# Six transfers of a gated attention and MLP kernel split by rows: 120 and 8, 8 and 56

## The chip, the cores and the metric

The kernel runs on one core of one Trainium2 chip. The core has five engines with an instruction stream each: TensorE (PE, with weight loads shown as PEld), VectorE (DVE), ScalarE (ACT), GpSimd (POOL) and SyncE (SP). Data goes between the chip's main memory (HBM) and the core's on-chip memory of 128 partitions in transfers that an engine's queue issues and that 16 DMA engines carry out. The metric is the time of one execution in device microseconds (us); lower is better.

## The reference

One token with 640 features goes through an attention block with 32 heads over a cache of 4,096 keys and values of 128 numbers, and through an MLP of 1,728 units with the mish activation. A gate mixes the two. What is wanted is the output and, for a given gradient of it, the gradients of x, of both caches, of both attention weights, of the MLP's three arrays and of the gate:

```python
def _fwd_reference(A_x, A_k_cache, A_v_cache, A_wq, A_wo, B_x, B_w1, B_b1, B_w2, gate_w):
    def _A_ref(x, k_cache, v_cache, wq, wo):
        B, Sq, D = x.shape
        H, Dh = 32, 128
        q = (x @ wq).reshape(B, Sq, H, Dh) -> (B, H, Sq, Dh)
        scores = jnp.einsum("bhqd,bhkd->bhqk", q, k_cache) * (Dh ** -0.5)
        p = _softmax(scores, axis=-1)
        o = jnp.einsum("bhqk,bhkd->bhqd", p, v_cache)
        return o -> (B, Sq, H * Dh) @ wo
    def _B_ref(x, w1, b1, w2):
        h = jnp.einsum("bsd,df->bsf", x, w1) + b1
        sp = jnp.log1p(jnp.exp(-jnp.abs(h))) + jnp.where(h > 0, h, jnp.zeros_like(h))
        return jnp.einsum("bsf,fd->bsd", h * jnp.tanh(sp), w2)
    g = _sigmoid((x * gate_w).sum(-1, keepdims=True))
    return g * _A_ref(...) + (1 - g) * _B_ref(...)

def reference(..., grad_out):
    out, vjp = jax.vjp(_f, A_x, A_k_cache, A_v_cache, A_wq, A_wo, B_w1, B_b1, B_w2, gate_w)
    return (out, *vjp(grad_out))
```

All arrays are bf16. Each head reads 1 MB of K and 1 MB of V and writes 1 MB of each one's gradient, 82.03 MB read and 82.03 MB written in all.

## The kernel before, in words

The work goes head by head, in an order written out by hand (the tile pools only hand out buffers and place the waits). A head's K and V lie as 128 partitions of 32 keys, 8,192 bytes to a partition. For a head h the loop turns V into its transposed form (`v_tr`: PE transposes of 128x128 into PSUM, ACT copies them out), works out the softmax and the gradient of the probabilities, turns K of head h+1 (`k_tr`), forms the gradient of V as an outer product on DVE (`dv_out`), then the scores of head h+1, and column sums over K and V (`dq_o`). The gradient of K follows one head later (`dk_out`). Both products go through the pool `outs` with four buffers `o_sb` of 1 MB, from which SP stores them.

K has four buffers and V three. So after `dq_o(h)`, which is the last to read the buffers of head h, `load_k(h + 4)` and `load_v(h + 3)` are issued. Nearly all transfers are issued by SP in the order of the program: in each head the two stores of products, the load of K, the load of V, and at some heads those of the weights wq and wo (in groups of four heads) and the stores of their gradients, which were written over the weights' own tiles. SP stands in this order: a transfer that has to wait holds up those behind it. Each transfer reports its landing on one of eight completion semaphores, which all HBM transfers of SP and ACT take in turn, so that a transfer also waits for the landing of the one that had its semaphore before.

The MLP's work is spread over the heads by a list with costs (`mq`). Its gradient of w2 (`dw2`) is written over the tile `w2_sb`: 13 columns of 128 rows, and 64 rows that are left over (F is 1,728 = 13 x 128 + 64). It is stored at head H - 4 = 28 in three pieces of 128 partitions and one piece of the 64 rows, 1,280 bytes each (line 725). The gradients of b1 (one row, `dh_bc`) and of w1 are stored at head 30, and three small stores of five rows each (`fin_rows`) end the kernel's compute, two of them issued by ACT and one by POOL. The last four stores are the halves of the two products of head 31, 512 KB each (line 580).

Lines of the page: L504 transposes, L505 copies from PSUM, L510 scores and gradient of the probabilities, L569 outer products, L582 their stores, L111 and L116 the loads of K and V, L592 column sums.

Of the kernel before, what the change touches and what calls it, by code (L numbers as in the profile page):

```python
# [16 lines left out]
def kernel(  # L17
# [24 lines left out]
    nc = tc.nc  # L42
    P = 128
    _, H, Sk, Dh = A_k_cache.shape
    D = A_x.shape[-1]
    F = B_w1.shape[1]
# [6 lines left out]
    FR = F // P  # L53
    FM = FR * P
    FT = F - FM
# [10 lines left out]
    Kv = A_k_cache.rearrange("b h (p j) d -> (b h) p j d", p=P)  # L66
    Vv = A_v_cache.rearrange("b h (p j) d -> (b h) p j d", p=P)
# [37 lines left out]

    kts, vts, wqs, wos = {}, {}, {}, {}

    def load_k(h):
        if h < H:
            kts[h] = kv_in.tile([P, J, Dh], BF16, name="Kn", tag="Kn")  # L110
            nc.sync.dma_start(kts[h][:], Kv[h])  # L111

    def load_v(h):
        if h < H:
            vts[h] = kv_in.tile([P, J, Dh], BF16, name="Vn", tag="Vn", bufs=VBUFS)
            nc.sync.dma_start(vts[h][:], Vv[h])  # L116

    wqp = {}

# [40 lines left out]
    w2_sb = const.tile([P, FCN, D], BF16, name="w2_sb")  # L160
# [83 lines left out]
    def g_do(g, hh):  # L244
        gp = groups[g]
        junk = small.tile([P, D], BF16, name="junk", tag="junk", bufs=2)
        nc.vector.scalar_tensor_tensor(junk[:], in0=wos[g][:, hh, :], scalar=1.0, in1=da_bc[:],  # L247
                                       op0=ALU.mult, op1=ALU.mult, accum_out=gp["do_col"][:, hh:hh + 1])
# [24 lines left out]
    def g_dobc(g):  # L273
        g_bcast(groups[g]["do_diag"], groups[g]["do_row"], 0, G)
# [16 lines left out]
    def f_bc(g, a=0, b=G):  # L291
        g_bcast(groups[g]["dq_diag"], groups[g]["dq_bc"], a, b)

    def f_o4(g):
        gp = groups[g]
        gp["o4"] = grp_sb.tile([P, G], F32, name="o4", tag="o4")
        ps = grp([P, G], F32, "o4_ps")
        nc.tensor.matmul(ps[:], lhsT=gp["o_sel"][:].rearrange("p h k -> p (h k)"), rhs=res[:], start=True, stop=True)
        nc.vector.tensor_copy(gp["o4"][:], ps[:])
        nc.vector.tensor_copy(gp["o_bf"][:], gp["o4"][:])  # L300
# [12 lines left out]
    def f_dx(g, c, a=0, b=G, slot=None):  # L313
        gp = groups[g]
        cs = slice(a * Dh, b * Dh)
        slot = g if slot is None else slot
        junk = small.tile([P, D], BF16, name="junk", tag="junk", bufs=2)
        nc.vector.scalar_tensor_tensor(junk[:, cs], in0=wqs[g][:, c, cs], scalar=1.0, in1=gp["dq_bc"][:, cs],  # L318
                                       op0=ALU.mult, op1=ALU.mult, accum_out=dx_parts[:, c, slot:slot + 1])
# [193 lines left out]
    def k_tr(h, c):  # L513
        if h < H:
            if c == 0:
                KT[h] = kvT.tile([P, J, P], BF16, name="KT", tag="KT")
            tr_block(kts[h], KT[h], c)

    def v_tr(h, c):
        if c == 0:  # L520
            VT[h] = kvT.tile([P, J, P], BF16, name="VT", tag="VT")
        tr_block(vts[h], VT[h], c)
# [11 lines left out]
    def softmax(h):  # L534
        mx = s_ps.tile([P, P + 2], F32, name="mx", tag="mx")
        nc.tensor.matmul(mx[:, 0:P], lhsT=scale_f[:], rhs=dgms.pop(h)[:], start=True, stop=True)  # L536
        negM = small.tile([P, 1], F32, name="negM", tag="negM")
        nc.vector.tensor_reduce(negM[:], mx[:, 0:P], axis=AX.X, op=ALU.max, negate=True)  # L538
        return mx, negM

    def exps(h, negM):
        es[h] = small.tile([P, J], BF16, name="e_bf", tag="e_bf")
        zds[h] = small.tile([P, 2], F32, name="zd", tag="zd")
        nc.scalar.activation(es[h][:], S_ps.pop(h)[:], ACT.Exp, bias=negM[:], scale=scale, accum_out=zds[h][:, 0:1])

    def dP(h):
        DP_ps[h] = s_ps.tile([P, J], F32, name="DP", tag="DP")
        cols_mm(DP_ps[h][:], VT.pop(h), doz[h // G % 2][:, h % G, :])
        pj = small.tile([P, J], F32, name="pj", tag="pj")
        nc.vector.scalar_tensor_tensor(pj[:], in0=DP_ps[h][:], scalar=1.0, in1=es[h][:],  # L550
                                       op0=ALU.mult, op1=ALU.mult, accum_out=zds[h][:, 1:2])

    def zd_mm(h, mx):
        nc.tensor.matmul(mx[:, P:P + 2], lhsT=ones_f[:], rhs=zds[h][:], start=True, stop=True)  # L554

    def probs(h, mx):
        rz = small.tile([P, 1], F32, name="rz", tag="rz")
        nc.vector.reciprocal(rz[:], mx[:, P:P + 1])
        negD = small.tile([P, 1], F32, name="negD", tag="negD")
        nc.vector.tensor_scalar(negD[:], mx[:, P + 1:P + 2], rz[:], -1.0, ALU.mult, ALU.mult)  # L560
        p4s[h] = p4b[h % 3][:, 0:J * 4].rearrange("p (j t) -> p j t", t=4)
        nc.vector.tensor_scalar(p4s[h], es.pop(h)[:].unsqueeze(2).to_broadcast([P, J, 4]), rz[:], None, ALU.mult)
        ds4s[h] = ds4b[h % 3][:, 0:J * 4].rearrange("p (j t) -> p j t", t=4)
        nc.vector.scalar_tensor_tensor(ds4s[h], in0=DP_ps.pop(h)[:].unsqueeze(2).to_broadcast([P, J, 4]),
                                       scalar=negD[:], in1=p4s[h], op0=ALU.add, op1=ALU.mult)
        zds.pop(h)
# [20 lines left out]
    def dk_out(h):  # L587
        out_pair(h, dKv, ds4s[h], groups[h // G]["qs_row"])
# [92 lines left out]
    for h in range(H - 1):  # L681
        g, hh = h // G, h % G
        nx, pv = g + 1 < NG, g > 0
        v_tr(h, 0)
        v_tr(h, 1)
        mx, negM = softmax(h)
        if h > 0:
            dk_out(h - 1)
        v_tr(h, 2)
        v_tr(h, 3)  # L690
        exps(h, negM)
        if hh == 0 and g == LG:
            g_dobc(g)
        dP(h)
        if hh == 0 and pv:
            f_o4(g - 1)
            f_bc(g - 1)
        k_tr(h + 1, 0)
        k_tr(h + 1, 1)
        zd_mm(h, mx)  # L700
        if hh == 0 and pv:
            f_dx(g - 1, 0)
        if hh == 1 and pv:
            f_dx(g - 1, 3)
        if hh == 2 and nx:
            g_do(g + 1, 0)
        if hh == 3 and nx:
            g_do(g + 1, 3)
        probs(h, mx)
        k_tr(h + 1, 2)  # L710
        if hh == 0 and pv:
            f_aT_pe(g - 1)
        k_tr(h + 1, 3)
        if hh == 3 and nx:
            g_dodiag(g + 1)
        dv_out(h)
        scores(h + 1)
        od = dq_o(h)
        load_k(h + KBUFS)
        load_v(h + VBUFS)  # L720
        if h == H - 4:
            assert dw2_next[0] == FCN
            for a, b in W2P:
                nc.sync.dma_start(dw2_v[:, a:b, :], w2_sb[:, a:b, :])
            nc.sync.dma_start(out_8[FM:F, :], w2_sb[0:FT, FR, :])
        if h == H - 2:
            assert not mq
            nc.sync.dma_start(db1_row, dh_bc[0:1, :])
            nc.sync.dma_start(dw1_v[:, 0:3, :], w1_sb[:, 0:3, :])
            nc.sync.dma_start(dw1_v[:, 3:RC, :], w1_sb[:, 3:RC, :])  # L730
        dqo_red(h, od)
        budget = 0.0
        if hh == 0:
            if nx:
                g_new(g + 1)
            if pv:
                f_aT_add(g - 1)
                f_dx(g - 1, 1)
                f_dx(g - 1, 2)
                f_dwo(g - 1, 0)  # L740
                f_dwo(g - 1, 1)
            budget = 0.9
        if hh == 1:
            if pv:
                f_dx(g - 1, 4)
                for c in range(RC):
                    f_dwq(g - 1, c)
                f_dwq_st(g - 1)
                f_dwo(g - 1, 2)
                f_dwo(g - 1, 3)  # L750
                f_dwo_st(g - 1)
            budget = 2.7
        if hh == 2:
            if nx:
                g_do(g + 1, 1)
                g_do(g + 1, 2)
                g_qcol(g + 1)
            budget = 0.9
        if hh == 3:
            if g % 2 == 0 and g + 2 < NG:  # L760
                load_wqp(g // 2 + 1)
            if g + 2 < NG:
                load_wo(g + 2)
            if nx:
                if g + 1 < LG:
                    g_dobc(g + 1)
                g_q(g + 1)
                g_qs(g + 1)
                g_docol(g + 1)
                f_new(g)  # L770
                f_diag(g)
            budget = 2.7
        if h >= 2:
            mlp_some(budget)
            dw2_some(2)

    g, h = NG - 1, H - 1
# [98 lines left out]
```

## Time and profile before

| | us |
|---|---|
| median of 3 runs | 415.16 (415.0 to 415.53) |
| the profiled execution | 416.13 |
| its span, first to last instruction | 414.4 |

| engine | busy us | share of the span |
|---|---|---|
| PE | 317.4 | 77% |
| DVE | 301.2 | 73% |
| ACT | 215.7 | 52% |
| POOL | 10.4 | 3% |

The granted clock of PE is 0.88 of full speed over the run. 164.05 MB go through SP's queue in the span. The 62 stores of whole products take 17.5 us (median) from issue to landing, the 32 loads of V 18.6, the loads of K 17.1. The longest waits of compute on a transfer: DVE's outer products on the stores that free their buffers 17.1 us in 10 waits, PE's transposes on V 3.5 us in 4 and on K 5.5 us in one, at the start.

How to read it: the page cuts the span into 40 slices of 10.36 us and gives for each the busy tenths of an engine, the share of the DMA engines in use and the GB/s that they moved. A queue's share is the time of its packets as a share of 16 engines' span. The chain of work that ended last goes back from the last instruction to what released it, step by step. In the timeline, a row is the start, the length and the instruction; SPq is SP issuing a transfer. Besides, the trace has for each completion semaphore the times of its single counts, and for every packet its start, length, size and queue; the number of the DMA engine is not in it.

### The profile page before, as it was taken

What the parts mean: (1) busy time and instruction counts of PE and PEld (TensorE: products, weight loads), DVE (VectorE), ACT (ScalarE), POOL (GpSimd) and SP (SyncE); (2) the same over time, 40 slices, a digit from 0 to 9 for tenths busy, and PEclk for the clock granted to TensorE, in tenths of its full rate; (3) what the DMA queues carried; (4) which work ended last, traced back from release to release, by engine and by line L of the source; (5) the groups of instructions that cost most, each with busy time, mean ns of one, the idle gap of its engine ahead of it and who ended that gap; (6) DMA issues with size and microseconds to landing.
All of it is one profiled execution on the core that took longest, in us unless ns stands there. A gap on an engine that the chain in (4) does not pass through costs nothing.

```text
span 414.4 us, 15457 instructions
## 1 busy us (share of the span) xinstructions
PE 317.4 (77%) x6839; PEld 285.2 (69%) x6839; DVE 301.2 (73%) x811; ACT 215.7 (52%) x447; POOL 10.4 (3%) x27
## 2 busy tenths in 40 slices
PE   4697995979859988888987876787978687879400
PEld 3497874878758886878777865777778685878400
DVE  2555872888689696999898885749899996886720
ACT  2364553755446445564567654774656445546600
POOL 3000001000000000000000002000000000000000
PEclk9998998989969798898989998987989898689855
DMA  8999999999999999999999999999999999999694
GB/s 273 406 413 422 419 422 422 407 420 419 421 421 420 418 419 421 411 420 419 422 420 423 416 404 411 409 417 423 422 416 375 411 394 414 403 391 377 278 346 168
DMA packets 31240, 165.05 MB, mean 398 GB/s; under 512 B 3012, under 2 KB 6725, under 8 KB 15174
## 3 DMA queue, kind: packets, MB, share of 16 engines
q1 hardware_dynamic: 30866, 164.05, 97.3%
q8 instruction: 53, 0.87, 0.8%
q14 instruction: 13, 0.11, 0.1%
q0 software_dynamic: 256, 0.01, 0.0%
q10 hardware_dynamic: 52, 0.01, 0.0%
HBM read 82.03 MB, written 82.03 MB: 396 GB/s over the span
## 4 chain that ended last, share of the span: by engine, by line
PE 32%; DMA 30%; DVE 17%; ACT 13%; issue 4%; DVEq 0%; ACTq 0%; SPq 0%
PE tr L504 14%; DMA out_dram<-o_sb 13%; DMA Vn<-in_A_v_cache_dram 10%; PE od L592 7%; DVE o_sb L569 6%; ACT KT L505 6%; DMA out_dram<-wo_g 5%; ACT VT L505 4%; PE DP L510 2%; PE S L510 2%; DVE junk L464 2%; PE q_ps L218 2%; DMA h_sb<-dh_bc 1%; DMA Kn<-in_A_k_cache_dram 1%; DVE junk L247 1%
## 5 line engine op out<-in xcount | busy, mean ns | idle before, releaser
L505 ACT COPY KT<-tr 128x512 f32<-128x512 f32 x128 | 69.8, 588 | 54.2 <-PE tr L504 54.1
L504 PE MATMUL tr<-ident_bf,Vn 128*128 128x128 bf16 x1024 | 80.3, 239 | 17.8 <-ACT VT L505 12.5
L504 PEld LDWEIGHTS <-Vn 128*128 128x128 bf16 x1024 | 71.8, 108 | 25.5 <-issue 20.1
L569 DVE TENSOR_TENSOR o_sb<-qs_row,ds 128x2048 bf16<-128x2048 bf16 x64 | 75.3, 1217 | 17.1 <-DMA out_dram<-o_sb 17.1
L505 ACT COPY VT<-tr 128x512 f32<-128x512 f32 x128 | 69.6, 584 | 27.4 <-PE tr L504 26.9
L504 PE MATMUL tr<-ident_bf,Kn 128*128 128x128 bf16 x1024 | 75.7, 230 | 7.0 <-DMA Kn<-in_A_k_cache_dram 5.5
L504 PEld LDWEIGHTS <-Kn 128*128 128x128 bf16 x1024 | 68.1, 105 | 12.0 <-DMA Kn<-in_A_k_cache_dram 5.5
L569 DVE TENSOR_TENSOR o_sb<-do_row,p 128x2048 bf16<-128x2048 bf16 x64 | 75.2, 1216 | 0.0
L532 ACT ACTIVATE dgm<-ident_bf,m 128x128 f32<-128x128 bf16 x32 | 12.9, 402 | 57.1 <-DVE m L530 57.1
L510 PE MATMUL DP<-doz,VT 128*128 128x32 bf16 x1024 | 36.3, 178 | 4.5 <-issue 2.1
L510 PE MATMUL S<-qz,KT 128*128 128x32 bf16 x1024 | 37.1, 180 | 3.1 <-ACT KT L505 0.4
L510 PEld LDWEIGHTS <-VT 128*128 128x128 bf16 x1024 | 31.7, 97 | 7.9 <-ACT VT L505 5.1
L510 PEld LDWEIGHTS <-KT 128*128 128x128 bf16 x1024 | 32.5, 98 | 6.5 <-ACT KT L505 5.6
L592 PE MATMUL od<-p,Vn 128*128 128x32 bf16 x1024 | 31.7, 179 | 3.7 <-issue 3.7
L554 PE MATMUL mx<-zd,ones_f 128*128 128x2 f32 x64 | 12.0, 258 | 25.9 <-DVE pj L550 25.7
L592 PEld LDWEIGHTS <-Vn 128*128 128x128 bf16 x1024 | 28.7, 97 | 4.1 <-issue 4.1
L592 PE MATMUL od<-ds,Kn 128*128 128x32 bf16 x1024 | 31.3, 180 | 0.1
L554 PEld LDWEIGHTS mx<-zd,ones_f 128*128 128x128 f32 x64 | 10.0, 197 | 28.8 <-DVE pj L550 28.8
L592 PEld LDWEIGHTS <-Kn 128*128 128x128 bf16 x1024 | 28.6, 98 | 0.2 <-issue 0.2
L247 DVE SCALAR_TENSOR_TENSOR junk<-wo_g,da_bc 128x640 bf16<-128x640 bf16 x32 | 25.4, 818 | 0.0
L318 DVE SCALAR_TENSOR_TENSOR junk<-wq_p,dq_bc 128x512 bf16<-128x512 bf16 x35 | 23.4, 684 | 0.7 <-ACT dq_bc L261 0.7
L538 DVE TENSOR_REDUCE negM<-mx 128x1 f32<-128x128 f32 x32 | 9.2, 286 | 17.5 <-PE mx L536 17.4
(162 smaller groups left out, 318.4 us busy)
## 6 DMA issues: line engine op xcount, KB each, us to landing
out_dram<-o_sb SPq DMA_DIRECT2D x62, 1024.0 KB, 17.5
Vn<-in_A_v_cache_dram SPq DMA_DIRECT2D x32, 1024.0 KB, 18.6
Kn<-in_A_k_cache_dram SPq DMA_DIRECT2D x31, 1024.0 KB, 17.1
wo_g<-in_A_wo_dram SPq DMA_DIRECT2D x8, 640.0 KB, 19.2
out_dram<-wo_g SPq DMA_DIRECT2D x7, 640.0 KB, 18.3
wq_p<-in_A_wq_dram SPq DMA_DIRECT2D x3, 1280.0 KB
out_dram<-wq_p SPq DMA_DIRECT2D x3, 1280.0 KB, 21.3
w_sb<-in_B_w_dram SPq DMA_DIRECT2D x1, 2160.0 KB
```

The lines of the kernel that those rows point to most:

```text
L218: nc.tensor.matmul(ps[:], lhsT=x_col_bf[:, rc:rc + 1].to_broadcast([P, P]), rhs=wqs[g][:, rc, :], start=(rc == 0), stop=(rc == RC - 1))
L247: nc.vector.scalar_tensor_tensor(junk[:], in0=wos[g][:, hh, :], scalar=1.0, in1=da_bc[:], op0=ALU.mult, op1=ALU.mult, accum_out=gp["do_col ...
L318: nc.vector.scalar_tensor_tensor(junk[:, cs], in0=wqs[g][:, c, cs], scalar=1.0, in1=gp["dq_bc"][:, cs], op0=ALU.mult, op1=ALU.mult, accum_ ...
L464: nc.vector.scalar_tensor_tensor(junk[0:n, :], in0=w2_sb[0:n, fc, :], scalar=dm[0:n, fc:fc + 1], in1=db_bc[0:n, :], op0=ALU.mult, op1=ALU. ...
L504: nc.tensor.transpose(tp[:, t, :], src[:, c * TB + t, :], ident_bf[:])
L505: nc.scalar.copy(dst[:, sl, :].rearrange("p a b -> p (a b)").bitcast(F32), tp[:].rearrange("p a b -> p (a b)").bitcast(F32))
L510: nc.tensor.matmul(out, lhsT=T[:, j, :], rhs=zrow[:, J - 1 - j:2 * J - 1 - j], start=(j == 0), stop=(j == J - 1))
L532: nc.scalar.activation(dgms[h][:], ident_bf[:], ACT.Copy, scale=m32[:])
L538: nc.vector.tensor_reduce(negM[:], mx[:, 0:P], axis=AX.X, op=ALU.max, negate=True)
L554: nc.tensor.matmul(mx[:, P:P + 2], lhsT=ones_f[:], rhs=zds[h][:], start=True, stop=True)
L569: nc.vector.tensor_tensor(dst[:, a:b, :].rearrange("p j (k t) -> p j k t", t=4), row.rearrange("p (k t) -> p k t", t=4).unsqueeze(1).to_br ...
L592: nc.tensor.matmul(out, lhsT=N[:, j, :], rhs=c4[:, 4 * j:4 * j + W], start=(j == 0), stop=(j == J - 1))
```

## The change

Two helpers load K and V. Both now go through a third one, which issues a load as one transfer of 128 partitions, or, for K of heads 8, 14, 20 and 26 and V of head 30, as two: partitions 0 to 119, and 120 to 127. The 64 rows at the end of dw2 are stored as 8 rows and 56 rows. Bytes, buffers and the order of all else stay as they are; SP issues six transfers more.

```diff
+    def load_rows(t, src, parted):
+        for a, e in ((0, P - 8), (P - 8, P)) if parted else ((0, P),):
+            nc.sync.dma_start(t[a:e, :, :], src[a:e, :, :])
+
     def load_k(h):
         if h < H:
             kts[h] = kv_in.tile([P, J, Dh], BF16, name="Kn", tag="Kn")
-            nc.sync.dma_start(kts[h][:], Kv[h])
+            load_rows(kts[h], Kv[h], h in (8, 14, 20, 26))
 
     def load_v(h):
         if h < H:
             vts[h] = kv_in.tile([P, J, Dh], BF16, name="Vn", tag="Vn", bufs=VBUFS)
-            nc.sync.dma_start(vts[h][:], Vv[h])
+            load_rows(vts[h], Vv[h], h in (30,))
...
             for a, b in W2P:
                 nc.sync.dma_start(dw2_v[:, a:b, :], w2_sb[:, a:b, :])
-            nc.sync.dma_start(out_8[FM:F, :], w2_sb[0:FT, FR, :])
+            for a, e in ((0, 8), (8, FT)):
+                nc.sync.dma_start(out_8[FM + a:FM + e, :], w2_sb[a:e, FR, :])
```

## The prediction

> **What bounds the kernel now.** I read the page's slices and queues first, then the chain that ended last, then the DMA view of the end, and at last the trace's record of completion counts and of single packets.
>
> ```profile
> span 414.4 us, 15457 instructions
> DMA  8999999999999999999999999999999999999694
> GB/s 273 406 413 422 419 422 422 407 420 419 421 421 420 418 419 421 411 420 419 422 420 423 416 404 411 409 417 423 422 416 375 411 394 414 403 391 377 278 346 168
> ...
> q1 hardware_dynamic: 30866, 164.05, 97.3%
> ```
>
> The transfers of SP's queue (q1) fill 97.3% of 16 engines' span, at some 420 GB/s until slice 23 and less after it. No compute engine is above 77%. The DMA engines bound the kernel, and something takes from them late.
>
> ```profile
> 233.96 19.49 DMA out_dram<-o_sb
> 268.12 18.88 DMA Vn<-in_A_v_cache_dram
> 305.68 19.64 DMA out_dram<-o_sb
> 327.85 20.44 DMA out_dram<-wo_g
> 348.35 21.34 DMA Vn<-in_A_v_cache_dram
> 379.42 15.35 DMA out_dram<-o_sb
> ```
>
> These are the longest pieces of the chain of work that ended last: start, length, what. From 234 us on it is made of transfers that take 15 to 21 us from issue to landing.
>
> ```profile
> DMA  9798899289994929999999999910000000000000
> GB/s 445 318 503 333 304 362 367 76 279 343 360 350 142 342 97 419 365 428 410 399 390 415 398 399 425 388 71 27 27 27 27 27 27 27 27 27 27 0 0 0
> ```
>
> This is the DMA view of the last 18.4 us alone (396.0 to 414.4), 0.46 us a slice. From slice 27 on 27 GB/s are moved. 420 / 16 is 26: **one** engine of the 16 still works, alone, for the last 5 us.
>
> The completion counts say how that came about. Every transfer of 128 rows gives 16 counts, one from each engine. The sixteenth comes 1.3 us behind the fifteenth at 126 us, 4.6 at 233, 8.95 at 369.7 (V of head 30: 360.74 and 369.69), and 4.91 at the last store (408.54 and 413.45). The gap grows mainly at stores, 0.1 to 0.35 us each, and hardly at loads (0.00 to 0.05), always for one and the same late engine. And this engine does not rest: from 5 us on its counts follow each other at its own service time (2.48 and 2.50 us for the last two stores of 1 MB, 1.22 to 1.26 for the four of 512 KB). So the end of the kernel is the late engine's work, added up. What the others do, and the compute, lies beside it.
>
> **The change part by part.**
>
> *Price of a row.* The first counts of successive 1 MB transfers lie 2.46 us apart for 8 rows per engine: 0.307 us a row of 8,192 bytes (a packet lasts 0.309). The packet that reports completion lasts 0.009. A transfer of one row per engine is then about 0.32 us. A packet of 1,280 bytes lasts 0.055.
>
> *How many engines a transfer uses.* The 128-row and 64-row transfers give 16 counts, the 5-row stores of fin_rows 5 (and one by the issuing queue), the one-row store of dh_bc 1 (and one). All fit the largest divisor of the rows that is not over 16. From these rows I read 15 engines for 120 rows (8 rows each, as now), 8 for 8 rows (one each), 14 for 56 (4 each, as now with 64 on 16). So every split takes 8 rows from one engine, gives one row more to eight others and leaves seven as they are.
>
> *Where the late engine stands.* The one-row store of dh_bc was issued at 386.25 and landed at 387.45, while the 1 MB store issued before it (383.35) had its sixteenth count only at 397.27: its row was not on the late engine. The first 5-row store (issued 394.70) started packets at 397.910, 397.923, 397.946, 398.011 and 398.103. The last one starts as a 3,456-byte packet of the late engine ends (397.970 to 398.106), and the next of that engine starts 15 ns later than its step of 132: this row was on the late engine. The second 5-row store shows the same (its completion packet at 399.517 stands between two packets of the late engine). So the late engine is used by 5 rows and not by 1. If the engines used for few rows are among those used for more, it is among the eight and among the fifteen, and gets one row more in each split.
>
> [...]
>
> *K of heads 8, 14, 20, 26 and V of head 30.* Added on the late engine: 5 x 0.32 = 1.60 us, nothing removed. All of it is on the path, as this engine has no idle time to put it in. Bounds from the rows: -2.46 each (it is the one left out) and +0.32 each; I take the upper, by the 5-row stores.
>
> *Tail of dw2.* Now 4 rows of 1,280 bytes per engine, 0.22 us with completion. After: 4 rows or none of the 56, and one or none of the 8: -0.22 to +0.065. I take +0.065 by the same argument.
>
> *The waits on SP.*
>
> ```profile
> 249.17 0.34 SPq L111 DMA_DIRECT2D Kn<-in_A_k_cache_dram  x1
> 250.92 0.34 SPq L116 DMA_DIRECT2D Vn<-in_A_v_cache_dram  x1
> 253.47 0.38 SPq L130 DMA_DIRECT2D wq_p<-in_A_wq_dram  x1
> ```
>
> Here SP issues (start, length). Eight completion semaphores are used in turn, so each transfer waits for the landing of the one eight places before it: 249.17 follows a landing at 249.10, 250.92 one at 250.86. The six added transfers each take a place. Behind a split K stands V of head 7, 13, 19 or 25, then the stores of the next products, and they wait for a landing one transfer later, up to 2.5 us; PE's transposes wait for both parts of a split tile, DVE for o_sb buffers behind the stores. An issue itself holds SP for 0.34 to 0.38 us. I cost all this at 0: at such an issue the late engine still has seven transfers queued, with a small one among them 6 x 2.46 + 0.32 = 15 us of work, and SP's hold-up doesn't starve it. Without that cover (a late engine that has caught up) a place would cost up to 2.5 us, 12 in all for the five. No gain can come from fewer places. PE, DVE and ACT keep their instructions: 0.
>
> *Sum.* 1.60 + 0.065 = 1.66 us. The profiled execution has span 414.4 in a run of 416.13 (1.7 outside); it becomes 416.1 and 417.8. The median of the runs shown, 415.16, is 0.97 below that run and becomes **416.8 us**, 0.4% slower. What a measurement can tell from no change is about 0.2%, 0.83 us.
>
> **The rivals.**
>
> *A: the late engine is the one that 120 rows leave out (faster).* Then it loses 5 x 2.46 + 0.22 = 12.5 us. It decides from the point where the fifteenth engine becomes last: at the dwq store issued at 375.09 the counts stand at 381.27 (fifteenth) and 390.72. Behind that store each engine has 22.7 us of work (1.55 + 2.46 + 2.46 + 3.18 + 2.12 + 2.46 + 1.26 + 1.70 + 0.42 + 4 x 1.26), so the fifteenth would end near 404.0, or 405.6 if it gets the extra rows, instead of 413.45: 405.7 to 407.3, taken as 406. If loads also come earlier and the waits of DVE and PE shrink, the tail could save some 3 us more. For it: such a split only helps then, and 12.5 is near the greatest gap of 13.6 us between first and last count. Against it: the 5-row stores.
>
> [...]
>
> *B: the late engine serves the 120 rows but not the 8 (no change).* For instance if engines for 8 rows are picked anew each time. Then 0 to +0.06: 415.2. The two 5-row stores that both hit it speak against a changing pick.
>
> *C: 120 rows go over 8 engines, 15 each (much slower).* Late engine: +8 rows per split, 5 x 2.46 = 12.3 us, 427.5. Against it: 5 counts for 5 rows, so the number isn't kept to powers of two.
>
> **How the numbers follow.** Forecast 0.57, A 0.30, B 0.10, C 0.03. A is not small, because the argument on nested sets of engines rests on stores of one and five rows, four of them on another queue, and nothing shows 120. The forecast alone spans 415.9 to 417.8 (1.66, with 0.3 for the spread of the runs and 0.6 for starved issues). Eight times in ten needs most of A: 405 to 418, which leaves out the fast part of A (0.09), C, and 0.03 above. Faster: A, 0.30. Same: B and a little of the forecast, 0.12. Slower: 0.58.
>
> **What would show it.** Right: split transfers with 15 and 8 counts, the sixteenth engine's gap as large as now at 369 us, a last stretch at 27 GB/s of 5 us or more, span 1.7 us up. A shows as no lonely engine at the end, landings near 17 us instead of 20 after 234 us. What would make the forecast wrong: a late engine that is another one in the timed runs than in this trace, or an order of engines for 120 rows that leaves out one which 5 rows use.

## The result and the profile after

The changed kernel takes 429.68 us (median of 4 runs, 427.11 to 430.97) where the kernel before takes 415.35 beside it: 1.0338 times as long, 95% interval 1.029 to 1.0387. That is 14.3 us slower. Forecast were 416.8 and a range from 405 to 418. (One execution of one kernel below, the cut into 112 and 16 rows, was in a slow state, 578.56 us; its time there is the median of the other three.)

The page of the changed kernel, the span, the DMA slices (10.7 us each) and SP's queue (packets, MB, share of 16 engines' span):

```profile
span 429.0 us, 15469 instructions
...
DMA  8999999999999999999999999999999999998794
GB/s 275 407 413 422 420 415 418 407 317 422 419 413 420 416 395 359 409 419 421 420 400 349 403 403 422 395 397 422 346 383 394 414 407 402 302 363 340 315 342 180
...
q1 hardware_dynamic: 30907, 164.05, 96.9%
```

Five places in the line of GB/s stand out: slice 8 (317, was 420), 14 and 15 (395 and 359), 21 (349), 28 (346) and 34 (302). They are the five split loads. The DMA line above stays at 9 there: the engines are as busy as ever and move less. The same shows in the queue's line: its bytes are 164.05 MB before and after, but 97.3% of 414.4 us is 403.2 us of work per engine and 96.9% of 429.0 us is 415.7. The engines work 12.5 us longer for the same bytes. A row more on some engines and a row less on others can't do that, because the mean over the engines doesn't move. So packets must have become longer.

The stretch of the first split, 86 to 95 us, by the DMA view. Before:

```profile
DMA packets 512, 3.75 MB, mean 417 GB/s; under 512 B 55, under 2 KB 55, under 8 KB 55
...
q1 hardware_dynamic: 511, 3.74, 99.7%
```

After:

```profile
DMA packets 375, 2.70 MB, mean 300 GB/s; under 512 B 47, under 2 KB 47, under 8 KB 47
...
q1 hardware_dynamic: 373, 2.67, 100.9%
```

Full engines, 28% fewer bytes. In the trace's record of single packets, those of 8,192 bytes that last over 500 ns are 182 of 16,000 before and 717 after; the normal one lasts 309.

The loss comes in five steps of 2.5 to 3.6 us, one at each split. Ahead of the first split the last counts of the changed kernel stand 0.2 us ahead of those of before (88.86 and 89.01 for the same store). Behind the five splits they stand 3.4, 6.1, 8.6, 12.0 and 14.6 us behind (119.65 and 116.25; 178.40 and 172.29; 251.88 and 243.28; 342.22 and 330.25; 392.07 and 377.49).

The end looks as it did. The DMA view of the last 18.4 us (410.6 to 429.0), 0.46 us a slice:

```profile
DMA  9897999129999908999999999950000000000000
GB/s 356 336 503 297 334 363 364 48 87 354 357 350 355 320 36 329 401 401 413 390 396 409 398 405 416 400 211 27 18 27 27 27 27 27 27 27 27 0 0 0
```

One engine alone at 27 GB/s again, from 423.30 (fifteenth count of the last store) to 428.01 (sixteenth). And the long transfers of the chain that ended last (start, length, what) have grown a little, from 15 to 21 us to 17 to 24:

```profile
285.50 22.83 DMA Vn<-in_A_v_cache_dram
312.61 20.10 DMA Vn<-in_A_v_cache_dram
334.53 20.64 DMA Vn<-in_A_v_cache_dram
355.23 23.66 DMA out_dram<-o_sb
378.91 16.75 DMA out_dram<-w_sb
```

### The profile page after: what moved, and what is told of

Its sections match the earlier page's. It is cut to its first block, busy times and chain, and to the rows that moved or that the text cites. A ratio compares the mean times of both kernels' runs of the same rounds, so it can differ in the third digit from the quotient of the medians.

```text
span 429.0 us, 15469 instructions
## 1 busy us (share of the span) xinstructions
PE 321.6 (75%) x6839; PEld 290.1 (68%) x6839; DVE 302.6 (71%) x811; ACT 217.3 (51%) x447; POOL 10.4 (2%) x27
## 3 DMA queue, kind: packets, MB, share of 16 engines
q1 hardware_dynamic: 30907, 164.05, 96.9%
## 4 chain that ended last, share of the span: by engine, by line
DMA 44%; PE 26%; DVE 13%; ACT 9%; issue 4%; DVEq 0%; ACTq 0%; SPq 0%
DMA out_dram<-o_sb 23%; DMA Vn<-in_A_v_cache_dram 15%; PE tr L508 12%; PE od L596 5%; DVE o_sb L573 5%; DMA out_dram<-w_sb 4%; ACT KT L509 4%; ACT VT L509 3%; PE S L514 2%; PE DP L514 2%; DVE junk L251 1%; PE q_ps L222 1%; DMA h_sb<-dh_bc 1%; DVE junk L468 1%; DMA Kn<-in_A_k_cache_dram 1%
## 5 line engine op out<-in xcount | busy, mean ns | idle before, releaser
L508 PE MATMUL tr<-ident_bf,Vn 128*128 128x128 bf16 x1024 | 81.3, 240 | 23.7 <-DMA Vn<-in_A_v_cache_dram 12.0
L508 PE MATMUL tr<-ident_bf,Kn 128*128 128x128 bf16 x1024 | 79.0, 235 | 7.2 <-DMA Kn<-in_A_k_cache_dram 5.4
L508 PEld LDWEIGHTS <-Kn 128*128 128x128 bf16 x1024 | 71.1, 108 | 12.4 <-DMA Kn<-in_A_k_cache_dram 5.4
L596 PEld LDWEIGHTS <-Kn 128*128 128x128 bf16 x1024 | 28.6, 98 | 0.6 <-issue 0.6
```

Source lines behind the costliest of these rows:

```text
L508: nc.tensor.transpose(tp[:, t, :], src[:, c * TB + t, :], ident_bf[:])
L596: nc.tensor.matmul(out, lhsT=N[:, j, :], rhs=c4[:, 4 * j:4 * j + W], start=(j == 0), stop=(j == J - 1))
```

## The theories

**Theory 1, a shared way.** The author's assumption, which the two traces don't show and the runs below test: in a transfer that is not of 128 rows, each engine holds consecutive partitions (8 of 120), and partitions 32 apart in the same half (0 to 63, or 64 to 127) lead by one way into the on-chip memory (SBUF), which passes one packet of 8,192 bytes in 0.309 us (the median of such a packet before). Engines whose partitions lie 32 apart in one half would then stand in each other's way. The 128-row form, whose packets do last 0.309 us, would have to deal its rows out so that this doesn't happen. Which engine holds which partition is not in any trace and stays assumed. What the runs below show of it is by partition: 32 rows on 0 to 31 take 1.28 us and 64 rows on 0 to 63 take 2.56, so 32 to 63 add no speed to 0 to 31, while 64 rows on 32 to 95 take 1.24. Partitions 64 to 127 as a whole were not run alone.

**Theory 2** is the forecast's price of a row, the same in any form. **Rivals** beside it: the six places that the added transfers take in the turn of the eight completion semaphores; the added row on the late engine alone; the tail of dw2.

## The experiments

### Rows alone

All computation and all other transfers are replaced by:

```
for a, e in ((0,128), (0,120), (0,112), (0,96), (0,64), (32,96), (0,32), (120,128), (0,128)):
    for i in range(10):
        t = kv_in.tile([P, J, Dh], BF16, ...)
        nc.sync.dma_start(t[a:e, :, :], Kv[i][a:e, :, :])
# then eight stores each of o[0:128], o[0:120], o[0:112]
```

> All computation is left out; only transfers of rows of 8,192 bytes are left, ten of a kind one behind the other: 128 rows, 120, 112, 96, 64 (partitions 0 to 63), 64 (partitions 32 to 95), 32 (0 to 31), 8 (120 to 127), 128 again; then stores of 128, 120 and 112 rows, eight of each. Theory 1 (a shared way into SBUF: in a form that is not of 128 rows each DMA engine holds consecutive partitions, and two engines whose partitions lie 32 apart then write by the same way, which passes one packet in 0.309 us): 128 rows 2.46 us a transfer; 120 rows between 2.5 and 4.9; 112 rows between 2.2 and 4.3; 96 rows at least 2.46; 64 rows on 0 to 63 2.46, but on 32 to 95 1.24; 32 rows 1.24; 8 rows 1.24. [...] Theory 2 (the price of a row is 0.31 us in any form, as the prediction had it): rows per engine times 0.309: 2.46, 2.46, 2.16, 1.85, 1.24, 1.24, 0.62 and 0.32. Theory 3 (the form of the transfer costs nothing in itself, the slow packets of the changed kernel come from what it does beside them): the same as theory 2.

The page of the one execution, slices of 7.6 us:

```profile
span 305.9 us, 160 instructions
...
DMA  7999999999999999999999999379999999999920
GB/s 289 427 421 342 210 212 215 213 224 234 271 279 283 266 251 247 251 216 196 208 205 240 419 279 201 65 207 425 424 410 429 429 380 376 393 283 285 304 96 37
```

128 rows run at 421 to 427 GB/s (slices 1 and 2), 120 rows at 210 to 224 (4 to 8): half. 64 rows on partitions 0 to 63 run at 205 to 208 (19 and 20), as many rows on 32 to 95 at 419 (22). A packet of 8,192 bytes lasts 309 ns (median) among the 128 rows, 611 among the 120, 641 on partitions 0 to 63 and 311 on 32 to 95. From the completion counts, us per transfer when they follow each other:

| rows | partitions | measured | theory 1 | theory 2 |
|---|---|---|---|---|
| 128 | 0–127 | 2.49 | 2.46 | 2.46 |
| 120 | 0–119 | 4.65 | 2.5–4.9 | 2.46 |
| 112 | 0–111 | 3.3 | 2.2–4.3 | 2.16 |
| 96 | 0–95 | 3.2 | ≥ 2.46 | 1.85 |
| 64 | 0–63 | 2.56 | 2.46 | 1.24 |
| 64 | 32–95 | 1.24 | 1.24 | 1.24 |
| 32 | 0–31 | 1.28 | 1.24 | 0.62 |
| 8 | 120–127 | 1.0–1.2 | 1.24 | 0.32 |

(120 rows: middle counts 32.64 to 69.85 us over eight transfers.) Theory 2 falls here: a row has not one price. Theory 1 holds in each line, within its range or to some 0.25 us. It also says why the loss is where the 120 rows are: 4.65 in place of 2.49 us.

### One part of the change at a time

The tail of dw2 alone, then the five loads alone:

```
-            nc.sync.dma_start(out_8[FM:F, :], w2_sb[0:FT, FR, :])
+            for a, e in ((0, 8), (8, FT)):
+                nc.sync.dma_start(out_8[FM + a:FM + e, :], w2_sb[a:e, FR, :])
```

> The kernel before with the tail of dw2 stored as 8 and 56 rows, nothing else. Forecast's step: +0.07 us. Theory 1 (shared way): 8 rows of 1,280 bytes on two ways, 4 packets of 0.055 us each, and 4 rows on each of 14 engines, at most twice 0.22 us: within +0.3. All theories: no difference that can be measured (415.2 within 0.8).

416.36 us, ratio 1.0012 (0.9996 to 1.0028): no difference that can be told.

> The five split loads alone, the tail of dw2 as before. Theories 1 (shared way) and 2 with the sizes of the changed kernel: all of the loss, 429 to 430 us (+14). If the tail of dw2 held a part of it, less by that part.

428.52 us, ratio 1.0303 (1.027 to 1.0337), 12.9 us over the 415.59 of before: the five loads carry nearly all of the loss.

### The same bytes, parted along the keys

```
-        for a, e in ((0, P - 8), (P - 8, P)) if parted else ((0, P),):
-            nc.sync.dma_start(t[a:e, :, :], src[a:e, :, :])
+        for a, e in ((0, J - 2), (J - 2, J)) if parted else ((0, J),):
+            nc.sync.dma_start(t[:, a:e, :], src[:, a:e, :])
```

> The same five loads, parted along the keys of a row in place of the partitions: 30 and 2 of the 32 keys of each partition, both on 128 partitions, so the same bytes, the same number of transfers, of issues and of completion semaphores used, and no engine with more rows than another. Theory 1 (shared way): no shared way, so near 415.2 plus the eight packets of 512 bytes more per engine and split, 5 x 8 x about 0.03 less what the 30 keys save (8 x 0.019 each): about +0.4. Rival, the places (six more transfers hold completion semaphores and SP issues later): as slow as the changed kernel, 427 to 431. Rival, the added row on the late engine alone: 415.2 to 416.

415.0 us, ratio 0.9982 (0.9969 to 0.9995). As many transfers, issues and places as the five loads of the changed kernel, the same 960 and 64 KB, and no loss. The line of GB/s has none of the five dips; from slice 1 to 34 nothing is under 394:

```profile
GB/s 266 408 414 419 421 419 423 407 417 420 420 424 397 403 419 411 410 424 418 421 420 409 419 417 424 411 420 423 413 417 414 412 394 402 424 403 374 311 336 170
```

The places are out as a cause. Parting along the partitions is the cause; the number of transfers isn't.

### Other cuts through the partitions

Only the bounds of the parts change: (0, 64, 128), (0, 112, 128) and (0, 32, 96, 128).

> The five loads parted into partitions 0 to 63 and 64 to 127. Every engine still has 8 rows of each tile, none more than another, and five transfers are added, as many as the 120 and 8 rows of the loads add. Rival (the loss is the row more that some engines get): no change, 415.6 within 0.8. Theory 1 (shared way): engines eight apart hold partitions 32 apart in both halves; 64 rows on 0 to 63 took 2.56 us alone where 128 rows took 2.49, so a split costs up to 2 x 2.56 - 2.49 = 2.6 us and the five 13, less where engines are at different transfers and don't meet: +6 to +13, 421 to 429.

> The five loads parted into 112 and 16 partitions: 16 engines with 7 rows and 16 with one, so the work of each engine is again 8 rows. Rival (the row more): no change, 415.6. Theory 1 (shared way), by the transfers alone: 112 rows took 3.3 us one behind the other, and 16 rows on 112 to 127 should take the 1.24 us that 32 rows and 8 rows took (four ways, 4 rows each); 3.3 + 1.24 - 2.49 = 2.05 a split, 10 in all: 421 to 426. Slower than before, less slow than the loads in 120 and 8 rows (428.5).

> The five loads parted into three, partitions 0 to 31, 32 to 95 and 96 to 127: ten transfers more than before, each on 16 engines. If added transfers or semaphore places cost the time, this is the slowest of these kernels, above 429. Theory 1 (shared way): 64 rows on 32 to 95 took 1.24 us alone, which is full speed, and 32 rows 1.28 in place of 0.62; 1.28 + 1.24 + 1.28 - 2.49 = 1.3 a split, 6.5 in all: 418 to 422, the least slow of the splits by partitions.

| parts of a tile | time | ratio (95%) | added, all five | by the transfers alone |
|---|---|---|---|---|
| 120 + 8 | 428.52 | 1.0303 (1.027–1.0337) | 12.9 | 5 x (4.65 + 1.2 - 2.49) = 16.8 |
| 64 + 64 | 425.9 | 1.0235 (1.0212–1.0258) | 9.8 | 5 x (2 x 2.56 - 2.49) = 13.2 |
| 112 + 16 | 425.67 | 1.0237 (1.0219–1.0256) | 9.6 | 5 x (3.3 + 1.2 - 2.49) = 10.1 |
| 32 + 64 + 32 | 419.32 | 1.0079 (1.0064–1.0094) | 3.2 | 5 x (1.28 + 1.24 + 1.28 - 2.49) = 6.6 |

(The kernel before took 415.59 us beside the first and 416.07 beside the others. 1.2 for 16 rows is from the crossed run below.) In the last three, by the author's reading of the counts (16 for 64 rows in the trace of before), every engine has 8 rows of each tile, as before; the rival of the added row forecast no change, and they lose 3 to 10 us. With three parts and ten transfers more, the cut that puts most rows on ways of their own loses least. Inside the kernel a split costs from half to nearly all of its price alone.

64 + 64 costs 9.8 us over five tiles, with 64 rows on 0 to 63 at half speed even alone (205 to 208 GB/s, where 128 rows run at 421 to 427).

Slices of 64 + 64 and of 32 + 64 + 32: the first split is again slice 8.

```profile
GB/s 279 403 414 422 423 416 422 408 323 421 423 419 420 416 404 350 407 424 420 422 419 347 339 410 420 413 409 419 393 336 391 420 399 404 366 406 372 328 346 176
```

```profile
GB/s 274 405 413 422 423 420 423 404 333 417 420 424 421 417 414 361 407 422 420 422 420 412 380 421 422 412 408 423 368 396 412 421 414 424 390 398 392 330 351 153
```

The first has the dips of the changed kernel at full size, though by that reading no engine got a row more (slices 8, 15, 21 with 22, 29); in the second the first is as deep and the later ones are shallower or shorter (361 in slice 15, 380 in 22, 368 in 28).

### One split alone

> K of head 8 alone in 120 and 8 rows. If the loss is a sum over the splits: a fifth of the 12.9 us that the five cost, 2.6, so 418.2 within 1.2. If it lies in the late splits, where the late engine is furthest behind: no difference, 415.6. If an early loss is made good later (the late engine rests somewhere behind it): no difference either.

417.72 us, ratio 1.0043 (1.0026 to 1.006): 1.65 us, where a fifth of 12.9 is 2.6. The counts don't show a cheaper split: K of head 8 lands at 94.25, before it landed at 91.44, and up to 315 us the last counts stay 2.2 to 3.3 us behind those of before. By the end that is 1.0 us. But the traces of before and of the dw2 tail alone, which run the same program up to the store at head 28, also part by 1.0 us between 317 and 333 us. So the loss adds up over the splits, and an early one costs about as much as a late one; how much of it reaches the end isn't settled to better than about 1 us.

### Partition or address?

So far row p of DRAM always went to partition p. This run crosses them:

```
lo, mid = slice(0, 64), slice(32, 96)
load(lo, lo); load(lo, mid); load(mid, mid); load(mid, lo)      # (partitions, rows), ten each
load(112:128, 112:128); load(120:128, 120:128)
load(64:96:4, 120:128); load(120:128, 64:96:4); load(0:128, 0:128)   # the last: six
```

> All computation is left out; only loads are left, ten of a kind one behind the other, with the rows in DRAM and the partitions in SBUF chosen apart. In this order: 64 rows on partitions 0 to 63 from rows 0 to 63; the same partitions from rows 32 to 95; partitions 32 to 95 from rows 32 to 95; the same from rows 0 to 63; 16 rows on 112 to 127; 8 rows on 120 to 127; 8 rows on 64, 68 ... 92 from rows 120 to 127; 8 rows on 120 to 127 from rows 64, 68 ... 92; six of 128 rows. If the shared way is in SBUF (by partition): 2.56, 2.56, 1.24, 1.24, 1.24, 1.05, 0.4 to 0.5 (an issue of SP takes 0.34 to 0.45, which is then the limit), 1.05. If it is in DRAM (by address, rows 256 KB apart): 2.56, 1.24, 1.24, 2.56, and 1.05, 1.05, 0.4 to 0.5 for the 8 rows. Mixed times would mean both.

The page of the one execution, slices of 3.4 us:

```profile
span 136.7 us, 131 instructions
...
GB/s 113 206 216 199 216 199 206 216 197 213 204 206 216 194 209 288 422 422 422 422 422 422 384 115 101 103 50 55 58 70 84 96 65 60 93 326 422 422 422 187
```

Slices 1 to 14 are partitions 0 to 63, from either set of rows: 2.53 us a transfer, no step between them. Slices 16 to 21 are partitions 32 to 95 from either set: 1.24. It is the partition that decides, not the address. 16 rows on 112 to 127 take 1.20 and move 109 GB/s, 8 rows on 120 to 127 take 1.20, from either set of rows, and move 55; on partitions four apart they take 0.67 where SP issues one each 0.67 us, so their own price is at most that. 207, 109 and 55 GB/s are what 8, 4 and 2 ways would give at 26 to 27.5 GB/s each, about the 26.5 of one packet of 8,192 bytes in 0.309 us. So the way belongs to the partitions; how a transfer deals its rows out to the engines stays assumed.

### What a row more costs where it shares no way

> The comparison for the next kernel. The five loads parted into 28 and 4 of the 32 keys of each partition, both on 128 partitions and 16 engines: 8 packets of 7,168 and 8 of 1,024 bytes on each engine. By the packets of before (1,024 bytes: 0.042 us) 0.34 + 8 x 0.27 = 2.50 in place of 2.46 a split, +0.2 in all. Parting into 30 and 2 keys stood at 415.0 beside 415.6: between 414.8 and 416.

414.88 us, ratio 0.9978 (0.9965 to 0.9992). (In the trace of before the 2,560 packets of 1,024 bytes take 0.046 us, median, not 0.042; by that the forecast would be 2.53 a split, +0.35 in all.) The kernel it was meant to be compared with, with rows of 1,024 bytes added on eight engines, gave no result; the next three took its place. Behind each K load of heads 6 to 29 they add two small loads into unused partitions:

```
+            if 6 <= h < 30:
+                for i in range(2):
+                    nc.sync.dma_start(w2_sb[ROWS, FR, :], Kv[h].rearrange("p j d -> p (j d)")[ROWS, 0:D])
# ROWS: 64 + i:65 + i   |   64 + i:96:4   |   112 + 8 * i:120 + 8 * i
```

> The kernel before with 48 transfers added, two behind each K load of heads 6 to 29, each of one row of 1,280 bytes into partitions that nothing uses. The places alone: 48 more semaphore places, 48 more issues, and one engine with 48 x 0.064 us more. The one-row store of dh_bc was not on the late engine, so by the prediction's reading the late engine gets nothing. If places cost nothing: 415.9 within 0.8. If a place costs what the prediction named as its price without cover, up to 2.5 us at times: well above 420.

> The same 48 transfers with 8 rows of 1,280 bytes each, on partitions 64, 68 ... 92 (and 65, 69 ... 93): 8 engines, no two of these partitions 32 apart. If the late engine is among the 8 and its work sets the end, as the prediction had it: 48 x (0.055 + 0.009) = +3.1 us, 419.0 within 0.8. If its work does not set the end, or it is not among the 8: as the kernel with one row.

> The same 48 transfers with 8 rows of 1,280 bytes on 8 neighbouring partitions, 112 to 119 and 120 to 127. Theory 1 (shared way): the 8 rows have two ways, four rows on each, and 8 neighbouring rows of 8,192 bytes took 1.05 to 1.2 us alone in place of 0.32, so a row of 1,280 bytes may take up to four times 0.055: between 419 (engines that are apart don't meet) and 426.5 (48 x 0.229 = 11). Rival (an added row has one price, wherever its partitions lie): the same as with partitions four apart.

| 48 transfers of | time | ratio (95%) |
|---|---|---|
| one row | 415.11 | 0.9983 (0.9972–0.9993) |
| 8 rows, four partitions apart | 419.55 | 1.009 (1.0071–1.0109) |
| 8 neighbouring rows | 418.39 | 1.0065 (1.0049–1.008) |

The bytes are few, and SP's queue is nearly as full with one row as with eight. One row, then eight rows four apart:

```profile
span 413.9 us, 15511 instructions
...
q1 hardware_dynamic: 30962, 164.11, 98.0%
```

```profile
span 418.4 us, 15511 instructions
...
q1 hardware_dynamic: 31634, 164.54, 97.8%
```

48 places and issues cost nothing. Seven rows more in each of the 48 transfers cost 4.4 us, against 3.1 forecast by 0.064 us a row; the neighbouring rows cost 3.3. The counts agree: late in the run the sixteenth count of the eight rows comes some 0.2 us behind that of the transfer ahead (322.24 and 322.00), the one row's long before (309.53 and 317.58). So the late engine is among the eight, its work moves the end, and the price of a row was right to within 1.07 to 1.45 times. The shared way did not show with these small rows: neighbours were even 1.2 us faster. The engines are far apart in time and a packet of 1,280 bytes lasts 0.055 us, so they may seldom meet; this is argued, not shown, and it leaves the 1.2 us open.

### Parting many loads along the keys

> Parting five loads into 30 and 2 keys stood 0.18% below the kernel before (interval 0.05 to 0.31%). Here all K loads from head 4 on and all V loads from head 4 on are parted so, 56 of them. If the small gain is a gain of each split: 5 gave 0.7 us, so 56 give several, 408 to 413. If it is chance: eight completion semaphores then cover 8 transfers of 0.5 MB on average among the loads, fewer bytes are under way, and the late engine gets 56 x 0.09 us (0.15 less than 8 packets of 0.03) of packets more: 416 to 425.

418.94 us, ratio 1.0067 (1.0047 to 1.0087). So what stood 0.2% below before with five loads isn't a gain of each split. 56 splits cost 3.0 us, less than the 5.0 (56 x 0.09) that the author estimated for the added packets on the late engine; the trace of before has no packet of 512 bytes to show that price.

## Why the prediction was wrong

- **The late engine sets the end: right.** It ends alone after the change as before it (4.71 and 4.91 us between the last two counts), and rows added to eight engines moved the end (419.55 us) where the same number of transfers with one row did not (415.11).
- **15, 8 and 14 engines, the late one among them: right.** The split loads give 15 and 8 counts and the dw2 tail 8 and 14, each with one more by the issuing queue. For V of head 30 the last two counts of the 120 rows are 375.27 and 383.85, and the last of the 8 rows comes at 384.18, 0.33 us behind on the same late engine: one row at its forecast price.
- **The price of a row: the step that failed.** "The first counts of successive 1 MB transfers lie 2.46 us apart for 8 rows per engine: 0.307 us a row" was read from transfers of 128 rows and then used for 120. From it followed "15 engines for 120 rows (8 rows each, as now)" at no cost. Those 8 rows take 4.65 us alone in place of 2.49. The term for the five loads was 1.60 us; it measured 12.9.
- **"What the others do, and the compute, lies beside it": wrong for the others.** Part of the loss fell on the late engine outside the split transfers. It wrote its 8 rows of V of head 30 at its normal pace (381.36 to 383.85, 2.49 us). Before that it had taken 4.00 and 4.61 us, in place of about 2.5, for two whole loads of 128 rows (365.28 to 373.89), while the other engines were in the split (their counts of the transfer ahead start at 365.65, those of the 120 rows run from 369.86 to 375.27). By theory 1 they then wrote by its way; no trace names the engines, so this is not shown. For K of heads 14, 20 and 26 its 8 rows took 4.1, 3.5 and 4.7 us.
- **The bounds of that term.** They ran from -2.46 to +0.32 a split: which engines get a row more or none. No bound was set for how long 8 rows take in a form of which the trace shows no instance. The nearest rows would have been the two transfers of 64 rows, of 80 KB each.
- **Places and SP's waits cost nothing: right.** Parting along the keys (415.0) and 48 one-row transfers (415.11) bear it out.
- **The tail of dw2, +0.065:** too small to be told from nothing, and no difference was measured.
- **The rivals.** A (the late engine left out, 406) and B (no change) fell with the counts. C gave 427.5, near the measured 429.7, but by 8 engines with 15 rows; there were 15 engines, and the time came from longer packets. That its number was close is chance. One reading beside them was off and does not change the sum: the greatest gap between first and last count is 14.4 us (310.87 and 325.32, the store issued at 305.68), not 13.6.

## What to carry to other kernels

Where a large load has to be cut, cut it along the free dimension, not along the partitions: here the same 960 and 64 KB cost nothing one way and 2.6 us a tile the other, while the DMA engines read as busy all along. A duration belongs to the form of the transfer it was read from (8 rows an engine took 2.49 us in the form of 128 rows and 4.65 in that of 120); where a change introduces a form that the trace lacks, set its upper bound by running the new form alone or by counting how many of its rows share a way, and look at GB/s beside the busy share, because here full engines moved 300 GB/s in place of 417 from 86 to 95 us, and packets of 8,192 bytes lasted 611 ns in place of 309 where 120 rows ran alone. Such a price can also fall on other transfers under way at the time, as it did on the late engine (4.00 and 4.61 us for loads of 128 rows, in place of about 2.5).

## What the runs showed of the hardware that was not expected

- 64 rows take 2.53 to 2.56 us on partitions 0 to 63 and 1.24 on 32 to 95, whatever rows of DRAM they come from.
- 120 rows take nearly twice as long as 128 as loads. As stores they share unevenly: the middle counts of eight stores in a row run from 251.06 to 269.63 us (2.65 each), the last ones from 251.57 to 285.87 (4.9 each), so some engines keep their speed and others lose half. In the loads the engines kept together: the counts of one transfer lie 0.6 to 0.8 us apart, early and late.
- Three kernels with added transfers for which no shared way showed (30 + 2 keys, 28 + 4 keys, 48 single rows) all stand 0.17 to 0.22% below the kernel before, each with an interval below 1 (28 + 4 keys: 0.08 to 0.35% below). 56 loads parted into 30 + 2 keys are slower than it. What the few gain is not known.
